# Row-tile outputs, a PSUM-held output sum, K scores ahead of V scores and a new order of transfers in an attention and feed-forward backward step

## The chip, the cores and the metric

One Trainium2 chip, one of its cores. The metric is the device time of one execution in microseconds; each quoted time is the median of several executions. The traced execution is a separate one, and its span lies some 1 to 5 us under the timed median. In what follows PE is the matrix engine, DVE and ACT are the vector and the scalar engine, and SP and Pool are the two engines that issue transfers here (Pool also does some small computation). PSUM is the memory that PE's products are written to; DVE and ACT copy them out of it (`evac` in the code).

## The reference

The forward pass is one decode step, one new token for each of four sequences, with attention over a sliding window of a cache and a GEGLU feed-forward block in parallel. The kernel computes the output and its gradients for x, both caches and all weights.

```python
# B=4, D=512, Hq=32, Hkv=8, Sk=4096, Dh=128, F=1792, W = 1024 (the window), bf16
xn = layernorm(x)
q  = (xn @ wq)                                    # 32 heads, 4 of them on each cached head
k, v = k_cache[:, :, Sk-W:], v_cache[:, :, Sk-W:]
o  = softmax(q k^T / sqrt(Dh)) v
y  = x + o @ wo + (gelu(xn @ w_gate) * (xn @ w_up)) @ w_down
# outputs: y, and the gradients for x, k_cache, v_cache, wq, wo, w_gate, w_up, w_down
```

The gradients of the caches have the full length of 4096 positions, but only the last 1024 are other than zero. So three quarters of dK and dV are plain zeros that the kernel has to write: 32 stores of 1536 KB, 50 MB of the 81 MB written.

## The kernel before

Attention runs in four rounds `t` of two cached heads each. In a round, K and V blocks are transposed on PE for the scores (`T_ps`, `S_ps`, `dP_ps`), a softmax follows, then o and dq (`od_ps`), the dV and dK products (`kv_ps`) with their stores, and the weight gradients dwo and dwq with theirs. The scores of round t+1 are computed between the dV and dK products and the weight gradients of round t. The order of SP's instructions is that of the program; the other engines' is the automatic scheduler's.

```python
# zeros and loads share SP's queue; each zero is held until a compute instruction is done
def zeros(n, after):
    for _ in range(min(n, len(zlist))):
        og, b, g = zlist.pop(0)
        z = nc.sync.dma_start(out=og[b, g:g + ZG, 0:K0, :]..., in_=zsrc)
        tc.add_manual_dep(z.ins, after.ins.name, ...)
...
def scores(t):                       # K and V together
    for b in range(B):
        for blk, nm in ((k_t[(t, b)], "k"), (v_t[(t, b)], "v")):
            ...  # 8 transposes into T_ps, ev = evac(T_sb, T_ps)
        zeros(1, ev)
        ...      # products into S_ps and dP_ps
...
def softmax(t):                      # one chain over both S_ps and dP_ps
    ...  # reduce_max -> PE (mT_ps) -> reduce_max -> PE (nm_ps) -> Exp, sums -> PE (tot_ps)
    ...  # -> P_b, dS_b -> PE (pT_ps) -> PT
...
def dvdk(t, stage):
    for src, mr, og, nm in ((P_b, domr, out_3, "dv"), (dS_b, qmr, out_2, "dk")):
        for g in range(GP):
            ...  # 8 products into kv_ps, ev = evac(stg, kv_ps)
            nc.gpsimd.dma_start(out=og[...], in_=stg[...])
        zeros(1, ev)
...
def fin(t):
    ao_ps = ps_x.tile([B, D], FP32, name="ao_ps", tag="x")       # sums on 4 partitions
    for h in range(HG):
        nc.tensor.matmul(ao_ps[:], lhsT=oT[:, h, :], rhs=wo_sb[:, h, :], start=(h == 0), stop=(h == HG - 1))
    nc.vector.tensor_tensor(out=acc_o[:], in0=ao_ps[:], in1=acc_o[:], op=ALU.add)
    ...  # transposes of o and dq to [4, 1024], the same for dxa_ps
    ...  # dwo and dwq products, contraction over 4 rows, stores on Pool
...
for t in range(NT):
    softmax(t)
    odq(t)
    ...  # loads for t+1 and t+2, pre(t+1)
    dvdk(t, stage)
    if t + 1 < NT:
        scores(t + 1)
    fin(t)
```

Of the kernel before, what the change touches and what calls it, by code (L numbers as in the profile page):

```python
# [13 lines left out]
P = 128  # L14
# [3 lines left out]
def kernel(  # L18
# [57 lines left out]
    ps_s = ctx.enter_context(tc.tile_pool(name="ps_s", bufs=1, space=bass.MemoryType.PSUM))  # L76
    ps_x = ctx.enter_context(tc.tile_pool(name="ps_x", bufs=2, space=bass.MemoryType.PSUM))
# [13 lines left out]
    x_b = const.tile([B, D], BF16, name="x_b")  # L91
    nc.sync.dma_start(out=x_b[:], in_=A_x.rearrange("b s d -> (b s) d"))
    dy_b = const.tile([B, D], BF16, name="dy_b")
    nc.sync.dma_start(out=dy_b[:], in_=grad_out.rearrange("b s d -> (b s) d"))
# [6 lines left out]
    nc.vector.memset(one_f[:], 1.0)  # L101

# [29 lines left out]
    x_f = const.tile([B, D], FP32, name="x_f")  # L132
    nc.vector.tensor_copy(out=x_f[:], in_=x_b[:])
    stats = const.tile([B, nc.vector.BN_STATS_DIM], FP32, name="stats")
    nc.vector.bn_stats(out=stats[:], in_=x_f[:])
    mv = const.tile([B, nc.vector.BN_AGGR_DIM], FP32, name="mv")
    nc.vector.bn_aggr(out=mv[:], in_=stats[:])
    eps_t = const.tile([B, 1], FP32, name="eps_t")
    nc.vector.memset(eps_t[:], eps)
    rstd = const.tile([B, 1], FP32, name="rstd")  # L140
    nc.scalar.activation(out=rstd[:], in_=mv[:, 1:2], func=ACT.Sqrt, bias=eps_t[:], scale=1.0)
    nc.vector.reciprocal(out=rstd[:], in_=rstd[:])
    xn_f = const.tile([B, D], FP32, name="xn_f")
    nc.vector.tensor_scalar(out=xn_f[:], in0=x_f[:], scalar1=mv[:, 0:1], scalar2=rstd[:, 0:1],
                            op0=ALU.subtract, op1=ALU.mult)
    xn_b = const.tile([B, D], BF16, name="xn_b")
# [4 lines left out]
    for src, dstT in ((dy_b, dyT), (xn_b, xnT)):  # L151
        tps = ps_x.tile([P, ND, B], BF16, name="tps", tag="x")
        for c in range(ND):
            nc.tensor.transpose(tps[:, c, :], src[:, c * P:(c + 1) * P], ident[0:B, 0:B])
        nc.vector.tensor_copy(out=dstT[:], in_=tps[:])


    acc_o = const.tile([B, D], FP32, name="acc_o")
    acc_d = const.tile([B, D], FP32, name="acc_d")
# [12 lines left out]
    def load_kv(t, bs):  # L172
        for b in bs:
            for d_, src, nm in ((k_t, A_k_cache, "kb"), (v_t, A_v_cache, "vb")):
                tl = kvp.tile([P, GP, J, Dh], BF16, name=nm, tag=nm)
                nc.sync.dma_start(
                    out=tl[:].rearrange("p g j d -> p g (j d)"),
                    in_=src[b, t * GP:(t + 1) * GP, K0:Sk, :].rearrange("g (m j) d -> m g (j d)", j=J))
                d_[(t, b)] = tl

# [4 lines left out]
    def zeros(n, after):  # L185

        zsrc = bass.AP(tensor=ztile.tensor, offset=ztile.offset, ap=[list(ztile[:].ap[0]), [0, ZG], [1, ZW]])
        for _ in range(min(n, len(zlist))):
            og, b, g = zlist.pop(0)
            z = nc.sync.dma_start(out=og[b, g:g + ZG, 0:K0, :].rearrange("g (m j) d -> m g (j d)", m=P), in_=zsrc)  # L190
            tc.add_manual_dep(z.ins, after.ins.name,
                              mybir.DependencyInfo(mybir.DependencyClass.Sync, mybir.DependencyReason.DATA))
# [4 lines left out]
    def pre(t):  # L197

        wo_sb, wq_sb = wo_t[t], wq_t[t]
        do_ps = ps_x.tile([P, HG, B], FP32, name="do_ps", tag="x")  # L200
        for h2 in range(HG // 2):
# [4 lines left out]
            woT = tsb.tile([P, 2, ND, P], BF16, name="woT", tag="wT", bufs=2)  # L206
            evac(woT[:], wT_ps[:], 1024, half=True)
            for i in range(2):
                for c in range(ND):
                    nc.tensor.matmul(do_ps[:, 2 * h2 + i, :], lhsT=woT[:, i, c, :], rhs=dyT[:, c, :],  # L210
                                     start=(c == 0), stop=(c == ND - 1))
        q_ps = ps_x.tile([P, HG, B], FP32, name="q_ps", tag="x")
        for h in range(HG):
            for c in range(ND):
                nc.tensor.matmul(q_ps[:, h, :], lhsT=wq_sb[:, c, h * Dh:(h + 1) * Dh], rhs=xnT[:, c, :],
                                 start=(c == 0), stop=(c == ND - 1))
        res = []
        for ps, sc, zt, nm in ((do_ps, None, dom_all[t % 2], "do"), (q_ps, scale, qm_all[t % 2], "qs")):
            xT4 = attw.tile([P, NQ, B, HG], BF16, name=nm + "T4", tag=nm + "T4")
            src = ps[:].rearrange("p h b -> p b h").unsqueeze(1).broadcast_to([P, NQ, B, HG])  # L220
            if sc is None:
                nc.vector.tensor_copy(out=xT4[:], in_=src)
            else:
# [3 lines left out]
            r_ps = ps_x.tile([P, P], BF16, name=nm + "r_ps", tag="x")  # L227
            nc.tensor.transpose(r_ps[:], xT4[:].rearrange("p q b h -> p (q b h)"), ident[:])
            r4 = attw.tile([P, Dh], BF16, name=nm + "_r4", tag=nm + "_r4")
            nc.vector.tensor_copy(out=r4[:], in_=r_ps[:])  # L230
            mr = attw.tile([P, GP, B, Dh], BF16, name=nm + "mr", tag=nm + "mr")
            nc.gpsimd.tensor_tensor(out=mr[:].rearrange("p g b d -> p (g b) d"),  # L232
                                    in0=r4[:].unsqueeze(1).broadcast_to([P, NS, Dh]),
                                    in1=msk[:].rearrange("p g b -> p (g b)").unsqueeze(2).broadcast_to([P, NS, Dh]),
                                    op=ALU.mult)
            res.append(mr)
        st[t] = res

    def scores(t):
        qm_f = qm_all[t % 2][:].rearrange("p s c -> p (s c)")  # L240
        dom_f = dom_all[t % 2][:].rearrange("p s c -> p (s c)")
        S_ps = ps_s.tile([P, WQ], FP32, name="S_ps", tag="S")
        dP_ps = ps_s.tile([P, WQ], FP32, name="dP_ps", tag="dP")
        for b in range(B):
            tiles = []
            for blk, nm in ((k_t[(t, b)], "k"), (v_t[(t, b)], "v")):
                for g in range(GP):
                    T_ps = ps_w.tile([P, J, P], BF16, name="T_ps", tag="w")
                    for j in range(J):
                        nc.tensor.transpose(T_ps[:, j, :], blk[:, g, j, :], ident[:])  # L250
                    T_sb = tsb.tile([P, J * P], BF16, name="T_sb", tag="T" + nm)
                    ev = evac(T_sb[:], T_ps[:].rearrange("p j m -> p (j m)"), 1024, half=True)
                    tiles.append(T_sb)
            zeros(1, ev)
            for i, (acc, lf) in enumerate(((S_ps, qm_f), (dP_ps, dom_f))):
                for g in range(GP):
                    s = b * GP + g
                    for q in range(NQ):
                        nc.tensor.matmul(acc[q * RG:(q + 1) * RG, :], lhsT=lf[:, s * RG:(s + 1) * RG],  # L259
                                         rhs=tiles[i * GP + g][:, q * WQ:(q + 1) * WQ],  # L260
                                         start=(s == 0), stop=(s == NS - 1), tile_position=(0, q * RG))
        st[t] += [S_ps, dP_ps]

    def softmax(t):
        domr, qmr, S_ps, dP_ps = st[t]
        m = attw.tile([P, 1], FP32, name="m", tag="m")
        nc.vector.reduce_max(out=m[:], in_=S_ps[:], axis=AX.X)
# [12 lines left out]
        sums = attw.tile([P, 2], FP32, name="sums", tag="sums")  # L280
        nc.scalar.activation(out=E_f[:], in_=S_ps[:], func=ACT.Exp, bias=negm[:, 0:1], scale=1.0,
                             accum_out=sums[:, 0:1])
        Gt = attw.tile([P, WQ], FP32, name="Gt", tag="Gt")
        nc.vector.tensor_tensor_reduce(out=Gt[:], in0=E_f[:], in1=dP_ps[:], scale=1.0, scalar=0.0,  # L284
                                       op0=ALU.mult, op1=ALU.add, accum_out=sums[:, 1:2])
        tot_ps = ps_x.tile([P, 2], FP32, name="tot_ps", tag="x")
        nc.tensor.matmul(tot_ps[:], lhsT=rsum[:].rearrange("p q r -> p (q r)"), rhs=sums[:], start=True, stop=True)  # L287
        rr = attw.tile([P, 1], FP32, name="rr", tag="rr")
        nc.vector.reciprocal(out=rr[:], in_=tot_ps[:, 0:1])
        cc = attw.tile([P, 1], FP32, name="cc", tag="cc")  # L290
        nc.vector.tensor_tensor(out=cc[:], in0=tot_ps[:, 1:2], in1=rr[:], op=ALU.mult)
        P_b = attw.tile([P, WQ], BF16, name="P_b", tag="P_b")
        nc.scalar.activation(out=P_b[:], in_=E_f[:], func=ACT.Copy, scale=rr[:, 0:1])
        nc.vector.scalar_tensor_tensor(out=Gt[:], in0=dP_ps[:], scalar=cc[:, 0:1], in1=E_f[:],
                                       op0=ALU.subtract, op1=ALU.mult)
        dS_b = attw.tile([P, WQ], BF16, name="dS_b", tag="dS_b")
        nc.vector.tensor_scalar(out=dS_b[:], in0=Gt[:], scalar1=rr[:, 0:1], scalar2=None, op0=ALU.mult)

        pT_ps = ps_x.tile([P, 2, JQ, P], BF16, name="pT_ps", tag="x")
        for i, src in enumerate((P_b, dS_b)):  # L300
            for jj in range(JQ):
                nc.tensor.transpose(pT_ps[:, i, jj, :], src[:, jj * P:(jj + 1) * P], ident[:])
        PT = attw.tile([P, 2, JQ, P], BF16, name="PT", tag="PT")
        evac(PT[:], pT_ps[:], 512, half=True)
        st[t] = [domr, qmr, P_b, dS_b, PT]

    def odq(t):
        domr, qmr, P_b, dS_b, PT = st[t]
        od_ps = ps_x.tile([P, 2, NS, rep], FP32, name="od_ps", tag="x")
        for i, blks in enumerate((v_t, k_t)):  # L310
            for b in range(B):
                for g in range(GP):
                    s = b * GP + g
                    for j in range(J):
                        q, jj = j // JQ, j % JQ
                        nc.tensor.matmul(od_ps[:, i, s, :], lhsT=blks[(t, b)][:, g, j, :],  # L316
# [288 lines left out]
```

## Time and profile before

| | before |
|---|---|
| time, median of the first 3 runs | 328.48 us |
| traced span | 325.5 us |
| PE busy | 243.0 us (75%) |
| bytes moved by DMA | 112.08 MB, mean 344 GB/s |
| DMA idle, summed over slices of 4 us | 37.5 us |

The profile's rows themselves are read in the prediction.

### The profile page before, as it was taken

To read this page: it belongs to the slowest core of one execution; us is meant where nothing else is said; L and a number is where in the kernel's file an instruction comes from. 1 tells how busy PE (TensorE), PEld (TensorE's weight loads), DVE (VectorE), ACT (ScalarE), POOL (GpSimd) and SP (SyncE) were. 2 spreads that over 40 slices of the span, in tenths; PEclk is the share of its full clock that TensorE was granted. 3 is DMA by queue.
4 is the path that set the end of the run, shared out by engine and by line. 5 is a ranking of instruction groups with operands and counts; after the bars stand their busy time and mean duration, and the time that the engine had idled before them with its cause. 6 is when DMAs were issued, how large, how long until landed. Compare 5 with 4: busy or idle time off the path is not lost.

```text
span 325.5 us, 6244 instructions
## 1 busy us (share of the span) xinstructions
PE 243.0 (75%) x2630; PEld 135.7 (42%) x2630; DVE 158.6 (49%) x308; ACT 131.2 (40%) x202; POOL 51.5 (16%) x76
## 2 busy tenths in 40 slices
PE   0459986677997999980529999926199999269990
PEld 0355542226875337720425167315151674142430
DVE  5134353554465574662105666703055766156684
ACT  3013353444552564451105545611065556135651
POOL 6000002221400520020003310110024101101111
PEclk9999996555797557975555559955575599555595
DMA  6999999688596999999999899999976999983726
GB/s 237 381 365 386 383 393 423 280 322 353 231 406 273 340 418 425 418 423 411 375 339 385 329 376 404 411 377 396 324 281 239 382 399 413 387 313 142 280 110 244
DMA packets 34411, 112.08 MB, mean 344 GB/s; under 512 B 1920, under 2 KB 7824, under 8 KB 34384
## 3 DMA queue, kind: packets, MB, share of 16 engines
q1 hardware_dynamic: 26576, 81.02, 65.1%
q0 software_dynamic: 7808, 30.67, 24.7%
q8 instruction: 20, 0.33, 0.4%
q14 instruction: 7, 0.06, 0.0%
HBM read 30.68 MB, written 81.01 MB: 343 GB/s over the span
## 4 chain that ended last, share of the span: by engine, by line
PE 57%; DMA 30%; issue 4%; ACT 4%; DVE 4%; SPq 0%; ACTq 0%; DVEq 0%; POOLq 0%
DMA wo_sb<-in_A_wo_dram 15%; PE T_ps L250 12%; PE kv_ps L337 11%; DMA wd_sb<-in_B_w_down_dram 5%; PE ao_ps L352 5%; DMA out_dram<-osb_o 4%; PE woT_ps L205 4%; DMA out_dram<-osb_d 3%; DMA out_dram<-osb_g 3%; PE dxf_ps L496 2%; PE wqT_ps L369 2%; PE od_ps L316 2%; PE dP_ps L259 2%; PE dxa_ps L374 2%; PE S_ps L259 2%
## 5 line engine op out<-in xcount | busy, mean ns | idle before, releaser
L88 ACT COPY T_sb<-T_ps 128x1024 bf16<-128x1024 bf16 x26 | 26.1, 1013 | 26.4 <-PE T_ps L250 26.4
L89 DVE COPY T_sb<-T_ps 128x1024 bf16<-128x1024 bf16 x38 | 25.8, 690 | 19.6 <-PE T_ps L250 19.3
L205 PE MATMUL woT_ps<-ident,wo_sb 128*128 128x128 bf16 x128 | 13.7, 282 | 16.1 <-DMA wo_sb<-in_A_wo_dram 16.1
L89 DVE CAST stg_dk<-kv_ps 128x512 bf16<-128x512 f32 x30 | 20.7, 691 | 9.8 <-PE kv_ps L337 9.5
L88 ACT CAST stg_dv<-kv_ps 128x512 bf16<-128x512 f32 x34 | 19.3, 588 | 14.5 <-PE kv_ps L337 14.3
L250 PE MATMUL T_ps<-ident,kb 128*128 128x128 bf16 x256 | 24.8, 247 | 0.0
L89 DVE CAST stg_dv<-kv_ps 128x512 bf16<-128x512 f32 x30 | 20.1, 688 | 8.8 <-PE kv_ps L337 8.5
L88 ACT CAST stg_dk<-kv_ps 128x512 bf16<-128x512 f32 x34 | 19.5, 587 | 10.7 <-PE kv_ps L337 10.1
L337 PE MATMUL kv_ps<-domr,P_b 32*128 32x512 bf16 x64 | 20.5, 562 | 0.9 <-DVE stg_dv L89 0.7
L337 PE MATMUL kv_ps<-qsmr,dS_b 32*128 32x512 bf16 x64 | 20.8, 600 | 0.0
L287 PE MATMUL tot_ps<-sums,rsum 128*128 128x2 f32 x8 | 2.0, 323 | 24.9 <-DVE sums L284 24.9
L250 PEld LDWEIGHTS <-kb 128*128 128x128 bf16 x256 | 17.9, 111 | 6.6 <-issue 4.2
L89 DVE CAST osb_q<-dwq_ps 128x512 bf16<-128x512 f32 x16 | 10.4, 683 | 19.9 <-DMA out_dram<-osb_o 19.4
L250 PE MATMUL T_ps<-ident,vb 128*128 128x128 bf16 x256 | 20.1, 240 | 0.0
L352 PE MATMUL ao_ps<-wo_sb,oT 128*4 128x512 bf16 x32 | 18.6, 589 | 0.0
L89 DVE COPY woT<-woT_ps 128x1024 bf16<-128x1024 bf16 x10 | 6.9, 692 | 23.5 <-PE woT_ps L205 23.0
L205 PEld LDWEIGHTS <-wo_sb 128*128 128x128 bf16 x128 | 11.1, 128 | 17.4 <-DMA wo_sb<-in_A_wo_dram 16.3
L250 PEld LDWEIGHTS <-vb 128*128 128x128 bf16 x256 | 18.0, 110 | 0.1
L88 ACT CAST osb_q<-dwq_ps 128x512 bf16<-128x512 f32 x16 | 8.8, 587 | 19.3 <-DMA out_dram<-osb_o 18.7
L88 ACT COPY woT<-woT_ps 128x1024 bf16<-128x1024 bf16 x6 | 6.1, 1012 | 25.6 <-PE woT_ps L205 22.3
L386 POOL DMA_DIRECT2D out_dram<-osb_o x8 | 6.0, 754 | 65.4 <-ACT osb_o L88 57.2
L232 POOL TENSOR_TENSOR domr<-do_r,msk 128x1024 bf16<-128x1024 bf16 x4 | 7.6, 1891 | 47.6 <-DVE do_r L230 47.6
(184 smaller groups left out, 420.3 us busy)
## 6 DMA issues: line engine op xcount, KB each, us to landing
out_dram<-ztile SPq DMA_DIRECT2D x32, 1536.0 KB, 14.4
kb<-in_A_k_cache_dram SPq DMA_DIRECT2D x16, 512.0 KB, 11.1
vb<-in_A_v_cache_dram SPq DMA_DIRECT2D x16, 512.0 KB, 11.1
out_dram<-stg_dv POOLq DMA_DIRECT2D x8, 1024.0 KB, 6.5
out_dram<-stg_dk POOLq DMA_DIRECT2D x8, 1024.0 KB, 8.8
wo_sb<-in_A_wo_dram SPq DMA_DIRECT2D x4, 1024.0 KB, 12.5
wq_sb<-in_A_wq_dram SPq DMA_DIRECT2D x4, 1024.0 KB, 20.2
out_dram<-osb_o POOLq DMA_DIRECT2D x8, 512.0 KB, 9.6
```

Of the source, the lines that this page charges most:

```text
L88: return nc.scalar.copy(out=out, in_=in_)
L89: return nc.vector.tensor_copy(out=out, in_=in_)
L205: nc.tensor.transpose(wT_ps[:, i, c, :], wo_sb[:, 2 * h2 + i, c * P:(c + 1) * P], ident[:])
L232: nc.gpsimd.tensor_tensor(out=mr[:].rearrange("p g b d -> p (g b) d"), in0=r4[:].unsqueeze(1).broadcast_to([P, NS, Dh]), in1=msk[:].rearra ...
L250: nc.tensor.transpose(T_ps[:, j, :], blk[:, g, j, :], ident[:])
L259: nc.tensor.matmul(acc[q * RG:(q + 1) * RG, :], lhsT=lf[:, s * RG:(s + 1) * RG], rhs=tiles[i * GP + g][:, q * WQ:(q + 1) * WQ], start=(s = ...
L316: nc.tensor.matmul(od_ps[:, i, s, :], lhsT=blks[(t, b)][:, g, j, :], rhs=PT[:, i, jj, q * RG + s * rep:q * RG + (s + 1) * rep], start=(j = ...
L337: nc.tensor.matmul(mps[:].rearrange("p b d -> p (b d)"), lhsT=src[rs, jj * P:(jj + 1) * P], rhs=mr[rs, g].rearrange("p b d -> p (b d)"), s ...
L352: nc.tensor.matmul(ao_ps[:], lhsT=oT[:, h, :], rhs=wo_sb[:, h, :], start=(h == 0), stop=(h == HG - 1))
L369: nc.tensor.transpose(wT_ps[:, i, c, :], wq_sb[:, c, h * Dh:(h + 1) * Dh], ident[:])
L374: nc.tensor.matmul(dxa_ps[:], lhsT=dqT[:, h, :], rhs=wqT[:, i, :], start=(h == 0), stop=(h == HG - 1))
L496: nc.tensor.matmul(dxf_ps[:], lhsT=srcT_b[:, fc, :], rhs=wgT[:, i, :], start=(w_ == 0 and fc == 0), stop=(w_ == 1 and fc == NF - 1))
```

## The change

Its intent, part by part:

- **o and dq as row tiles:** the products that give o and dq put their rows on 128 partitions (four groups of 32, four rows used in each), where before they gave columns that had to be transposed to 4 partitions.
- **Masked full-array products:** dwo, dwq and the feed-forward weight gradients contract over 128 rows, with all rows but the four wanted ones masked to zero in `xnm` and `dym`.
- **Output sums in PSUM:** the sums for y and dx stay in one PSUM tile `acc_ps` to the end of the kernel, in products of 4 columns.
- **K scores, then V:** the softmax is cut in two, so that P and the o products need not wait for the V scores.
- **Transfers:** SP only loads. The zeros go to Pool's queue, in program order among the stores, without a gate of their own. Two of them wait for the last V load of round 0.

The transposes of w_gate and w_up now come behind the weight-gradient products of the feed-forward part; before, they came first. Besides, the pool `ps_x` of small PSUM tiles goes from two buffers to one, and x and dy are loaded 32 times over, on 128 partitions.

```diff
 def zeros(n, after=None):
-            z = nc.sync.dma_start(out=og[b, g:g + ZG, 0:K0, :]..., in_=zsrc)
+            z = nc.gpsimd.dma_start(out=og[b, g:g + ZG, 0:K0, :]..., in_=zsrc)
 ...
-        load_kv(0, range(B))
-        load_kv(1, range(2))
-        load_w(1)
+        last = load_kv(0, range(B))
+        load_w(1)
+        load_kv(1, range(2))
+        zeros(2, last)
 ...
+        def ftb(name):
+            t_ = ffn.tile([P, 4 * NF4, B], BF16, name=name)
+            nc.gpsimd.memset(t_[:], 0.0)
+            return t_
 ...
+    def acc_add(o, c, lhsT, rhs):
+        nc.tensor.matmul(acc_ps[:, o, c, :], lhsT=lhsT, rhs=rhs, start=False, stop=False)
 ...
-            nc.tensor.matmul(ao_ps[:], lhsT=oT[:, h, :], rhs=wo_sb[:, h, :], start=(h == 0), stop=(h == HG - 1))
+            for c in range(ND):
+                acc_add(0, c, wo_sb[:, h, c * P:(c + 1) * P], oT[:, h // rep, h % rep, :])
 ...
-                nc.tensor.matmul(mps[:], lhsT=o_bp[:, h * Dh:(h + 1) * Dh], rhs=dy_b[:], start=True, stop=True)
+                nc.tensor.matmul(mps[:], lhsT=o_r[:, g, :], rhs=dym[:, i, :], start=True, stop=True)
 ...
         pre(0)
-        scores(0)
+        masks(0)
+        scores(0, 0)
+        softmax(0)
+        scores(0, 1)
+        softmax_d(0)
         for t in range(NT):
-            softmax(t)
-            odq(t)
+            odq(t, 0)
+            odq(t, 1)
 ...
-            dvdk(t, stage)
-            if t + 1 < NT:
-                scores(t + 1)
+            dvdk(t, 0, stage)
+            if nxt:
+                scores(t + 1, 0)
+                softmax(t + 1)
+            dvdk(t, 1, stage)
+            if nxt:
+                masks(t + 1)
+                scores(t + 1, 1)
+                softmax_d(t + 1)
             fin(t)
 ...
+        zeros(len(zlist))
```

## The prediction

> **What bounds the kernel now.** I read first the slices of the page, to see which unit is full when; then the totals of the DMA queues; then the chain that ended last; then the busy table by stage, cut where the chain changes its kind.
>
> ```profile
> span 325.5 us, 6244 instructions
> ...
> PE   0459986677997999980529999926199999269990
> ...
> PEclk9999996555797557975555559955575599555595
> DMA  6999999688596999999999899999976999983726
> GB/s 237 381 365 386 383 393 423 280 322 353 231 406 273 340 418 425 418 423 411 375 339 385 329 376 404 411 377 396 324 281 239 382 399 413 387 313 142 280 110 244
> DMA packets 34411, 112.08 MB, mean 344 GB/s; under 512 B 1920, under 2 KB 7824, under 8 KB 34384
> ```
>
> The PE row has holes (the 0, the 2, the 1) where the DMA row is at 9. The DMA row has holes of its own: at the start, in slices 8 to 13 (56 to 104 us), near slice 31, and in the last five. 112.08 MB at the 344 GB/s mean is the span; at the 390 to 420 of full slices it would be 267 to 287 us. So the transfers are the floor, and the loss is the time in which they are not fed.
>
> ```profile
> DMA wo_sb<-in_A_wo_dram 15%; PE T_ps L250 12%; PE kv_ps L337 11%; DMA wd_sb<-in_B_w_down_dram 5%; PE ao_ps L352 5%; DMA out_dram<-osb_o 4%; PE woT_ps L205 4%; DMA out_dram<-osb_d 3%; DMA out_dram<-osb_g 3%; PE dxf_ps L496 2%; PE wqT_ps L369 2%; PE od_ps L316 2%; PE dP_ps L259 2%; PE dxa_ps L374 2%; PE S_ps L259 2%
> ```
>
> The largest member of the chain is the load of wo, 15% of 325.5 = 49 us: two pieces, 25.3 us from 143.5 and 23.8 us from 211.4 in the chain by time. The wo of the round after next stands on the one SP queue behind eight zero stores of 1536 KB each.
>
> ```profile
> 2.50:48.00 45.50, 30.91 (x409) 19.86 (x409) 17.54 (x47) 12.11 (x15) 3.51 (x13) 1.00 1.05 375
> 48.00:80.00 32.00, 22.65 (x105) 9.79 (x104) 14.89 (x26) 13.96 (x24) 7.52 (x12) 0.54 0.85 344
> 80.00:112.00 32.00, 29.64 (x508) 21.21 (x505) 17.95 (x42) 14.59 (x22) 6.40 (x5) 0.77 0.82 313
> 112.00:143.00 31.00, 30.52 (x284) 16.48 (x284) 19.37 (x31) 17.15 (x25) 4.89 (x6) 0.78 1.03 418
> 143.00:169.00 26.00, 7.26 (x143) 5.53 (x142) 4.60 (x14) 3.24 (x8) 2.18 (x3) 0.50 1.00 380
> ...
> 288.00:325.50 37.50, 29.39 (x244) 12.06 (x244) 23.20 (x41) 16.99 (x30) 5.95 (x8) 0.59 0.55 203
> ```
>
> Columns: stretch, length, busy us of PE, PE weight load, DVE, ACT, POOL, then granted clock, DMA share, GB/s. From 143 to 169 PE works 7 of 26 us, yet DMA is at 1.00: PE waits for wo, but those bytes (zeros) have to go out at some time anyway. Only the shares under 1 are true loss. Summed over slices of 8 us, 1 minus the share comes to some 39 us, of which about 18 are after 288 us, some 20 between 56 and 104. **The bound is the DMA stream and how it is fed**, not PE's 75%.
>
> **What the skill says.** "DMA: Bandwidth & Descriptors", section "Issuing engines are not separate DMA queues": transfers of SP and GpSimd run on the same 16 engines and interleave; a second issuer saves only issue time. So moving the zeros to Pool buys no bandwidth, only a different order. The trace agrees: the two queues took 65.1% and 24.7% for 81.02 and 30.67 MB, the same share per byte. "TensorE: Matmul & The Clock Gate", section "LDWEIGHTS (loading the stationary operand)": weight time follows the columns, not the rows. Agrees: 4x128 weights of xn_b take 106 ns where 128x128 take 104 to 111, so a masked product with all 128 rows costs no more than its 4-row form. The same page, Part 1: the default clock is half, and activity releases it. The trace has 1.00 in the dense start and 0.50 in the stretches where PE waits; I take no saving from it, as those are not PE's to set. "PSUM — Partial Sum Buffer", "The four PSUM rules": matmuls without the first flag keep adding to a written element, which lets one bank hold both sums to the end; no run here tests it.
>
> **The change part by part.**
>
> *Output sums.* ao, dxa, dxf and fo are 32+32+28+14 products with 512 moving columns: in the chain by time ao takes 0.52 us each, the others 0.26. That is 16.6 + 8.3 + 7.3 + 3.6 = 36 us. In their place come 4 products of 4 columns each, 424 in all, at the pace of the 128 od products (3.46 us, 27 ns): 12 us. About 24 us off PE. Eight DVE adds of 0.67 us (5 us) go too.
>
> *Row tiles.* The 64 + 42 transposes of tq and tf and their copies on 4 partitions (up to 1.0 us each, some 12 us over DVE and ACT) go; 16 transposes, 48 small products and small copies come. Some 7 us off PE. dwo, dwq, dwd and dwg keep their moving columns and their evacuations (0.59 us ACT, 0.68 DVE). od stays at 64 issues a side.
>
> Together about 30 us of PE work and 15 us of evacuation go, but nearly all of it in rounds that end waiting for transfers, so it is not 30 us of time.
>
> *Order of transfers.* The bytes stay at about 112.4 MB (the x and dy broadcasts add 0.25). Three things move:
> 1. Loads are alone on SP. wo of round t is now read early in the PE order, so the next wo leaves well ahead. The 49 us of PE waits go; PE then waits for store buffers instead, where it outruns the DMA.
> 2. Two zeros at the start wait for the last V load of round 0. They sit on the in-order Pool queue, and **the three memsets of aT_b, dhuT_b and dhgT_b sit behind them**. From the issue times before (one 512 KB load per 1.36 us) that load lands at about 36 us; so the FFN products start at about 40 us, not at 27 as their operands would let them (before, dwd started at 46).
> 3. Zeros stand between stores. None can leave while Pool waits for the next store, so between the last FFN store and the first dV store **nothing feeds the DMA**.
>
> *Time line.* (a) Loads on SP: 16.5 MB at 375 GB/s from 2.5 us: to 46.5. (b) Behind them 2 zeros (3.15 MB), FFN stores (5.5 MB) and 6 zeros (9.4 MB): 18 MB at 420, as full store slices show: 43 us, to 90 us. (c) PE is held by the three output buffers: its 12th FFN tile may fill once the 9th has landed, 13.6 MB into (b), at 79 us. From there it has the last transposes of w_up (5 us), pre(0) (5), scores (14 for K and V before, 81.7 to 95.5), the two softmax parts (6, part hidden), od (3): about 33 us, to 112. The DMA is empty from 90 to 112: **a 22 us hole**. (d) From 112 the remaining 77.5 MB. At 387 (time-weighted mean of the four stretches from 112 to 235 us) 200 us, less 3 because the last round's 15.7 MB are stores alone at 420: 197. (e) Inside the rounds compute and DMA are close: 22 MB or 56 us of DMA against some 45 to 50 us of compute; I allow 2 us for gaps. (f) 2 us for the last landing. Sum 112 + 197 + 2 + 2 = 313 us of span.
>
> A check from the other side: idle before about 39; after it 2.5 + 22 + 2 + 2 = 28.5, so 325.5 - 10.5 = 315. The timed runs lie 3.0 above the traced span (328.48 against 325.5), so 313 gives 316; I choose **315**, since the end of the last round may be fed better than I allowed.
>
> **Rivals.**
> *The hole is filled or shorter* (PE reaches dV sooner because the full-row products hold the clock at 1.00 and 30 us of work is gone): for it, slices 0 to 6 ran at 1.00 with dense work; against it, PE is held by the output buffers until 79 us whatever its speed. A hole of 8 us gives 301.
> *The in-order Pool queue becomes the bound*: every store waits for all ahead of it, zeros included, with 3 output and 4 stage buffers. For it, the chain already has out_dram<-osb_o at 4%, osb_d and osb_g at 3% each, with one zero now between. Against it, a wait behind a zero is time in which DMA works. If each round loses 4 us to it: 329.
> *The gain of PE is passed on in full* (if PE were the bound, 49 + 30 us: 250): against it, 112.4 MB in 250 us would need 450 GB/s and no full slice shows more than 425.
> *Compute bounds the rounds*: splitting the softmax in two adds a dependency chain (E_f, rr, P_b, then Gt, cc, dS_b). At 56 us a round: 325.
>
> **Range and chances.** The floor, with 2.5 us of start and no hole, is 112.4 MB / 397 (full slices) = 283 + 5, and 291 timed; I don't believe in it, as the hole follows from the queue order. Low 300 (half the hole), high 328 (rounds lose another 3 us each). Over 2% faster means under 321.9: 0.72. Within 2%: 0.22. Slower: 0.06.
>
> **What would show each step.** The chain no longer has 15% of wo loads, and PE's wait for wo is near 0. Sum products of 4 columns cost about 27 ns each. Pool's memsets of aT_b end at 35 to 40 us, and dwd starts after 38. The DMA row has a hole of two or three slices between 85 and 115 us, and is at 9 from there to the end, where slices 36 to 40 were 2 to 8. PE's waits move to the osb buffers, that is to stores behind zeros. The prediction is wrong if the hole is absent, if full slices run below 370 GB/s with the zeros on the software queue, if the rounds after 112 us show DMA gaps of over 10 us in all, or if Pool's issues take much more than the 0.75 us of before.

## More of the kernel before

The trace gives the mean busy share of the 16 DMA engines for any stretch; I cut the span into slices of 4 us, the last one ending with the span, and add up (1 minus the share) times the length, counting shares over 1 as 1. It says how long the DMA engines stood unfed.

(The idle times and the "281 us" that some expectations quote were summed with a last slice that ran past the end of the span, by up to 3.8 us.)

## The result and the profile after

The changed kernel is correct and **slower**: 338.97 us median (337.38 to 340.69, 4 runs) against 328.21 us (327.5 to 328.7) on the same chip. The ratio is 1.0331, with a 95% interval of 1.0275 to 1.0386. A ratio here is the mean time of one kernel's fast runs over that of the other's of the same rounds, so not quite the ratio of the medians.

From the page of the changed kernel: span, busy tenths and bytes in 40 slices of 8.4 us, the two DMA queues, and the chain that ended last.

```profile
span 335.5 us, 6853 instructions
...
PE   1352182477977899698669689768959988990020
...
DMA  5999999997900079887999999599998938999995
GB/s 175 395 361 385 373 417 418 420 417 312 411 26 2 12 259 380 352 337 301 350 415 418 416 413 410 216 358 416 417 419 347 395 149 325 376 395 403 405 389 211
...
q0 software_dynamic: 16512, 81.01, 59.9%
q1 hardware_dynamic: 18120, 30.94, 26.3%
...
PE T_ps L279 13%; DMA out_dram<-osb_o 12%; PE kv_ps L374 10%; PE S_ps L284 4%; DMA wq_sb<-in_A_wq_dram 4%; DMA out_dram<-osb_g 4%; DMA vb<-in_A_v_cache_dram 3%; PE wqT_ps L395 3%; PE woT_ps L233 3%; SPq L193 3%; PE acc_ps L146 3%; DMA out_dram<-osb_d 3%; PE wgT_ps L555 3%; PE od_ps L348 3%; DVE T_sb L90 2%
```

The 15% of wo loads are gone from the chain, the tail of the DMA row is all but full (slices 36 to 40 were 2 to 8 before), and a hole of three slices stands at 92 to 118 us. All of this was foreseen. What was not are the weak places among the rounds: slices 17 to 19, 26, 31, 33 and 34. The idle DMA time is 51.1 us against 37.5 before, 13.6 more, and the span is 10.0 longer.

Pool's timeline of the changed kernel shows the hole from the side of the issuer. Columns: start, duration, engine, line, operation, count; in brackets how long Pool waited before it, and for what.

```profile
38.89 1.59 POOL L217 DMA_DIRECT2D out_dram<-ztile  x2 [33.11 <-DMA vb<-in_A_v_cache_dram]
40.48 0.17 POOL L458 MEMSET aT_b<- 128x64 bf16 x1
...
84.37 0.71 POOL L217 DMA_DIRECT2D out_dram<-ztile  x1
...
123.92 0.80 POOL L378 DMA_DIRECT2D out_dram<-stg_dv  x1 [26.04 <-ACT stg_dv L89]
...
142.44 0.78 POOL L378 DMA_DIRECT2D out_dram<-stg_dk  x1 [8.10 <-ACT stg_dk L89]
...
159.98 0.79 POOL L409 DMA_DIRECT2D out_dram<-osb_o  x1 [8.74 <-ACT osb_o L89]
```

The last zero of the feed-forward part leaves at 84.4 and the first dV store at 123.9. Between them Pool issues no transfer at all, though 24 zeros are still in its program: each stands behind a store that is not ready. After that the three groups of stores of round 0 are 18.5 and 17.5 us apart.

### The profile page after: what moved, and what is told of

Read it like the earlier page. It is cut to its first block, busy times and chain, and to the rows that moved or that the text cites. A ratio compares the mean times of both kernels' runs of the same rounds, so it can differ in the third digit from the quotient of the medians.

```text
span 335.5 us, 6853 instructions
## 1 busy us (share of the span) xinstructions
PE 223.8 (67%) x2956; PEld 142.8 (43%) x2956; DVE 154.4 (46%) x304; ACT 127.7 (38%) x203; POOL 74.3 (22%) x111
## 4 chain that ended last, share of the span: by engine, by line
PE 50%; DMA 26%; DVE 9%; ACT 5%; SPq 4%; issue 3%; POOL 1%; ACTq 0%; DVEq 0%; POOLq 0%
PE T_ps L279 13%; DMA out_dram<-osb_o 12%; PE kv_ps L374 10%; PE S_ps L284 4%; DMA wq_sb<-in_A_wq_dram 4%; DMA out_dram<-osb_g 4%; DMA vb<-in_A_v_cache_dram 3%; PE wqT_ps L395 3%; PE woT_ps L233 3%; SPq L193 3%; PE acc_ps L146 3%; DMA out_dram<-osb_d 3%; PE wgT_ps L555 3%; PE od_ps L348 3%; DVE T_sb L90 2%
## 5 line engine op out<-in xcount | busy, mean ns | idle before, releaser
L90 DVE COPY T_sb<-T_ps 128x1024 bf16<-128x1024 bf16 x40 | 27.7, 692 | 31.5 <-PE T_ps L279 31.3
L89 ACT COPY T_sb<-T_ps 128x1024 bf16<-128x1024 bf16 x24 | 24.3, 1012 | 31.2 <-PE T_ps L279 25.0
L217 POOL DMA_DIRECT2D out_dram<-ztile x32 | 22.8, 714 | 50.1 <-DMA vb<-in_A_v_cache_dram 33.1
L279 PE MATMUL T_ps<-ident,vb 128*128 128x128 bf16 x256 | 24.4, 258 | 0.0
L374 PE MATMUL kv_ps<-qmr,dS_b 32*128 32x512 bf16 x64 | 22.6, 596 | 0.3
L89 ACT CAST stg_dk<-kv_ps 128x512 bf16<-128x512 f32 x33 | 18.9, 587 | 7.1 <-PE kv_ps L374 6.7
L279 PEld LDWEIGHTS <-kb 128*128 128x128 bf16 x256 | 18.9, 115 | 5.3 <-issue 3.1
L374 PE MATMUL kv_ps<-domr,P_b 32*128 32x512 bf16 x64 | 18.6, 528 | 2.1 <-DVE stg_dv L90 0.8
L378 POOL DMA_DIRECT2D out_dram<-stg_dv x8 | 6.2, 775 | 45.6 <-ACT stg_dv L89 44.0
L600 PE MATMUL f_ps<-ident_f,acc_r 128*128 128x128 f32 x8 | 2.0, 428 | 20.3 <-ACT osb_q L89 20.3
L378 POOL DMA_DIRECT2D out_dram<-stg_dk x8 | 6.2, 779 | 40.0 <-ACT stg_dk L89 28.9
L233 PEld LDWEIGHTS <-wo_sb 128*128 128x128 bf16 x128 | 10.2, 119 | 10.5 <-issue 10.3
L89 ACT CAST osb_d<-dwd_ps 128x512 bf16<-128x512 f32 x8 | 4.6, 587 | 25.4 <-PE dwd_ps L529 18.6
```

Of the source, the lines that this page charges most:

```text
L89: return nc.scalar.copy(out=out, in_=in_)
L90: return nc.vector.tensor_copy(out=out, in_=in_)
L217: z = nc.gpsimd.dma_start(out=og[b, g:g + ZG, 0:K0, :].rearrange("g (m j) d -> m g (j d)", m=P), in_=zsrc)
L233: nc.tensor.transpose(wT_ps[:, i, c, :], wo_sb[:, 2 * h2 + i, c * P:(c + 1) * P], ident[:])
L279: nc.tensor.transpose(T_ps[:, j, :], blks[(t, b)][:, g, j, :], ident[:])
L374: nc.tensor.matmul(mps[:].rearrange("p b d -> p (b d)"), lhsT=src[rs, jj * P:(jj + 1) * P], rhs=mr[rs, g].rearrange("p b d -> p (b d)"), s ...
```

## The experiments

Where only the zeros or the program order were edited, the automatic scheduler also moved some instructions of PE, DVE and ACT. All results were correct. The same-round kernel before had medians of 328.15, 326.64, 327.19 and 327.29 us in the four batches, which ran on three chips; so a difference between runs of different batches is good to some 1.5 us. For e4, e6, e9 and e14 the interval of the ratio contains 0.98 but ends below 1: they are faster than before, by about 2%.

| run | what it is | median us | ratio to before | span | DMA idle us |
|---|---|---|---|---|---|
| before | | 328.21 | 1 | 325.5 | 37.5 |
| after | the change | 338.97 | 1.0331 | 335.5 | 51.1 |
| e1_fill | after, six zeros moved into the hole | 332.72 | 1.0138 | 330.2 | 44.1 |
| e2_memset | after, memsets ahead of the two zeros | 339.10 | 1.0350 | 336.2 | 51.8 |
| e3_oldqueue | compute of after, zeros on SP with gates | 327.27 | 0.9981 | 323.3 | 37.3 |
| e4_newqueue_before | compute of before, transfers of after | 322.63 | 0.9828 | 321.8 | 39.2 |
| e5_dxfirst | e2, w_gate and w_up transposes first | 337.62 | 1.0312 | 335.9 | 51.0 |
| e6_kvtogether | after, K and V scores together | 320.95 | 0.9806 | 317.7 | 36.5 |
| e7_both | e5 and e6 | 313.86 | 0.9586 | 312.5 | 31.5 |
| e8_bothfill | e7, eight zeros moved into the hole | 314.27 | 0.9605 | 313.2 | 29.0 |
| e9_beforefill | e4, the same move | 320.19 | 0.9758 | 318.2 | 32.9 |
| e10_splitspread | after, a zero of each pair held to mid-scores | 338.71 | 1.0333 | 335.5 | 50.7 |
| e11_best | e7, seven zeros in the hole, the others regrouped | 304.01 | 0.9279 | 301.5 | 18.9 |
| e12_oldq_together | e3, K and V scores together | 314.25 | 0.9575 | 309.7 | 25.2 |
| e13_joinstores | after, dV and dK side by side, chain in the middle | 338.04 | 1.0288 | 336.4 | 53.8 |
| e14_movechain | after, softmax moved behind the V scores | 319.35 | 0.9754 | 316.8 | 36.0 |

### First batch: the hole, the memsets, and compute against queue order

Theory H: the hole after the feed-forward part costs the time, and the order of transfers is at fault. Its rivals were that Pool's single queue binds (P), and that the new compute does (C).

**e1_fill**

```diff
-            if f4 % 2: zeros(1)             # and the same among the w_gate, w_up stores
+        zeros(1, ev)                        # after the last w_up transpose
+            if t == 0 and h2 == 1: zeros(1, ev)                    # in pre
+                if t == 0 and b % 2 and g == GP - 1: zeros(1, ev)  # in scores
```

> The changed kernel, with the six zero stores that stood between the FFN stores moved into the stretch of round 0 without any store (one behind the last w_up transpose, one in pre(0), four in the scores of round 0, each gated on an evacuation). Theory H (the hole between the last FFN store and the first dV store, about 27 us with a DMA share near 0, sets the loss): the FFN buffers come free some 15 us sooner (6.3 MB less ahead of the 9th store, at 0.42 MB per us) and the hole is mostly filled, so 320 us, between 315 and 326, against 339. Rival P (the zeros between the stores of the rounds hold the in-order Pool queue, the hole only lies beside it): 333 or more.

Measured 332.72 us, 1.0138 (1.0087 to 1.019). It falls between the two: 6 us came back, not enough to reach the kernel before. The trace shows that the run moved the hole more than it filled it: from 88 to 124 us the idle DMA time fell from 25.0 to 6.0 us, but from 56 to 84, where the six zeros had been, it rose from 1.9 to 13.4. So e1 doesn't say what a filled hole is worth, and it leaves open whether the hole makes the change a loss; e4 settles that.

**e2_memset**

```diff
+        for name in ("aT_b", "dhuT_b", "dhgT_b"):
+            t_ = ffn.tile([P, 4 * NF4, B], BF16, name=name)
+            nc.gpsimd.memset(t_[:], 0.0)
         zeros(2, last)
```

> The changed kernel, with the three memsets on Pool ahead of the two zeros that wait for the last V load. Theory H: the FFN products start some 13 us sooner, but the stores stay behind the same zeros and the DMA is full until 72 us anyway, so under 4 us is gained: 335 to 339. Rival M (the late FFN start is handed on to everything after it): 326, that is 13 us less.

Measured 339.10 us, 1.035 (1.0285 to 1.0414). The memsets behind the zeros really held PE for 12.9 us, and it cost nothing: the products for y that use `aT_b` start at 27.0 us instead of 41.0, but the first dV store leaves at 124.3 where it was 123.9.

**e3_oldqueue**

```diff
-            z = nc.gpsimd.dma_start(out=og[b, g:g + ZG, ...
+            z = nc.sync.dma_start(out=og[b, g:g + ZG, ...
-                evac(stg[:, :, j, :], mps[:], 512)
+                ev = evac(stg[:, :, j, :], mps[:], 512)
-            zeros(1)
+        zeros(1, ev)               # and the other gates as in the kernel before
```

> The computation of the changed kernel, with the zeros on the SP queue behind gates on evacuations, 8 a round and 5 in the FFN, as in the kernel before; Pool has only stores. Theory H (the order of transfers is at fault, the new computation saves some time): no hole, 318 us, between 312 and 325, under the 328 of before. Rival C (the new computation is at fault, by its split softmax and its longer PE order): 335 or more, like the changed kernel.

Measured 327.27 us, 0.9981 (0.9918 to 1.0044). Neither theory: the new compute under the old queue order gains nothing and loses nothing.

**e4_newqueue_before**

```diff
-            z = nc.sync.dma_start(out=og[b, g:g + ZG, ...
+            z = nc.gpsimd.dma_start(out=og[b, g:g + ZG, ...
-            zeros(1, ev)
+                zeros(1)           # one behind each store, as in the changed kernel
+    def masks(t):                  # the mask products leave pre: Pool's order is now fixed
```

> The computation of the kernel before, with the transfers of the change: loads alone on SP, the zeros on Pool between the stores in the same places, two behind the last V load (this kernel has no memsets behind them). Theory H: it gets the hole and the short round gaps too, 345 us, between 338 and 355, slower than before by 3% or more. Rival C (the order of transfers is harmless or good): 330 or less.

Measured 322.63 us, 0.9828 (0.9773 to 0.9883). H is refuted: the new order of transfers alone makes the old compute 1.7% faster, hole and all (its slices 12 and 13 moved 22 and 2 GB/s, and it has 19.8 us of idle DMA from 88 to 124). So the loss is in the compute part, or in how the two go together.

### Second batch: which part of the compute

Theory R: two things delay the stores. One is that the w_gate and w_up transposes stand behind buffer-bound products, so the first dV store is late; the other is the split of K and V.

**e5_dxfirst**

```diff
+        for srcT, wsb in ((dhgT_b, wg_sb), (dhuT_b, wu_sb)):
+            ...                    # transposes and acc_add(1, ...), moved up unchanged
         def f_rows(srcT, nm):
-            for f2 in range(NF // 2):
-                ...                # from behind the w_gate and w_up stores
```

> The kernel of e2 (memsets ahead of the zeros), and the transposes of w_gate and w_up with their sums put ahead of the FFN weight gradients, as in the kernel before, in place of among and behind them. Theory T (what the change lost is the time to the first dV store, as nothing is sent until then and some 214 us follow it in the changed kernel, in e1 and in e4; a part of that delay is the PE work that waits behind FFN products held by the output buffers): round 0 starts some 8 us sooner, 331 us, between 327 and 334. Rival R (the time after the first dV store is what counts, and takes up any shift): 337 to 341, like e2.

Measured 337.62 us, 1.0312 (1.0277 to 1.0347). The first dV store leaves at 119.7 instead of 123.9, but the next round's at 180.4, where it was 179.8: the rounds swallow the gain.

**e6_kvtogether**

```diff
-        scores(0, 0); softmax(0); scores(0, 1); softmax_d(0)
+        scores(0, 0); scores(0, 1)
         for t in range(NT):
+            softmax(t)
+            softmax_d(t)
 ...
-                scores(t + 1, 0); softmax(t + 1)
             dvdk(t, 1, stage)
-                masks(t + 1); scores(t + 1, 1); softmax_d(t + 1)
+                masks(t + 1); scores(t + 1, 0); scores(t + 1, 1)
```

> The changed kernel with K and V scores together and the two softmax parts after both, as before. Theory T: the chain of the first softmax part stands between the K and the V transposes on the in-order PE, and the stage from the wo transposes to the first dV product takes 33 us against 24.5 in e4; undone, the first dV store comes about 8 us sooner and the rounds are not longer: 330 us, between 324 and 334. Rival R (the split costs nothing, since V transposes run beside the chain): 336 or more.

Measured 320.95 us, 0.9806 (0.9767 to 0.9844). 18 us came back by the order of the calls alone: same instructions, same transfers. The first dV store is where it was (124.0 against 123.9), so an earlier first store is not the reason; the gain lies in the rounds.

**e7_both**

> e5 and e6 in one: what is left of the change is row tiles, masked products, the one PSUM accumulation and the queue order. Theory T: the two delays add up, and the first dV store comes as early as in e4 or a few us sooner: 320 us, between 313 and 326, within 2% of e4's 322.6. Rival A (the row tiles, masked products or PSUM sums cost time themselves): 330 or more, clearly above e4.

Its edit is the two above together. Measured 313.86 us, 0.9586 (0.9539 to 0.9632). With the rounds repaired, the feed-forward order that was worth nothing in e5 is worth 7 us (e6 to e7).

**e8_bothfill**

```diff
+                if t == 0 and g == GP - 1: zeros(1, ev)     # in scores
-        zeros(1)                   # the two in fin
```

> e7, with eight zeros moved out of the rounds (the two of each fin) into the scores of round 0, each behind an evacuation there. Theory T: the hole of some 25 us gets 12.6 MB (30 us of DMA) that the rounds then lack, so 300 us, between 292 and 308. Rival B (the rounds are bound by the computation, so bytes taken from them buy nothing): 315 or more.

Measured 314.27 us, 0.9605 (0.9567 to 0.9642), a miss. The hole shrank from 22 us to 6, but the zeros taken from `fin` left new gaps ahead of the dV stores and at the end: from 140 to 280 us the idle DMA time rose from 2.0 to 12.5.

### Third batch: where zeros are of use, and the split under the old queue

**e9_beforefill** (the edit of e8 on e4)

> e4 (the computation of before, the transfers of the change) with the two zeros of each round's fin moved into the scores of round 0, as e8 has them against e7. e8 gained nothing (314.3 against 313.9): it closed the hole of round 0 but had new gaps before the dV stores and at the end, as fin no longer has a zero. Theory G (the span is 281 us, give or take 4, of full transfers plus the time in which the DMA is not fed, whatever the computation): e9 too wins the hole and loses it in the rounds: 318 to 325. Rival (a filled hole is worth its length): 303.

Measured 320.19 us, 0.9758 (0.9695 to 0.9821), 2.4 us under e4: inside the range of theory G and far from the rival's 303.

**e10_splitspread**

```diff
+                if t > 0 and b == 1 and g == GP - 1: zeros(1, ev)   # in scores
-            zeros(1)
+            if g == 0 or t == NT - 1: zeros(1)
```

> The changed kernel, K then V kept, with one of the two zeros behind each pair of dV stores and of dK stores held back until the middle of the K scores and of the V scores of the next round (gated on an evacuation). Theory G: the round gaps of the split (about 16 us of DMA idle between 136 and 280 us) come from the queue running dry while PE does scores and softmax; spread zeros fill them: 325 us, between 319 and 330. Rival S (the split's softmax chain on the PE order sets the rounds, and the gaps only show it): 335 or more.

Measured 338.71 us, 1.0333 (1.028 to 1.0385): nothing. That is in the range of rival S, but it was a poor test, as I saw in the trace. The second zero of the dV pair already left late in the changed kernel (at 133.6), so my gate moved the same bytes in the same order by a few microseconds.

**e11_best**

```diff
+            if t == 0 and h2 == 1: zeros(1, ev)                                 # in pre
+                if t == 0 and g == GP - 1 and (k == 0 or b < 2): zeros(1, ev)   # in scores
-            zeros(1)               # behind each dV and dK store
+            if t + 1 < NT: zeros(1)
-        zeros(1)                   # in fin, behind the dwo stores
-        zeros(1)                   # in fin, behind the dwq stores
+        zeros(1 if t + 1 < NT else len(zlist))
```

> e7 with seven zeros in the hole (one in pre(0), six in the scores of round 0), one zero behind the last store of each fin but the last, and in the last round none between the stores and two behind all of them. Theory G: the hole is closed and neither the rounds nor the end run dry; DMA idle falls from 35 to about 14 us: 298 us, between 291 and 306. Rival S (the rounds are bound by computation): 310 or more.

Measured **304.01 us**, 0.9279 (0.9224 to 0.9334), which beats both kernels. Its page, busy tenths of DMA and GB/s in 40 slices of 7.5 us:

```profile
DMA  5999999999998999996999999999999999679696
GB/s 151 399 350 384 381 386 418 422 422 417 414 417 338 400 425 380 361 416 277 340 400 418 412 348 359 422 418 393 411 406 405 421 414 406 241 308 362 250 349 266
```

No empty slice is left. What remains lies in the first slice, slice 19 and the last six; 18.9 us of idle DMA against 31.5 in e7.

**e12_oldq_together** (the edit of e6 on e3)

> e3 (the computation of the change, zeros on SP behind gates as before) with K and V scores together. Theory S (the split lengthens the PE path of each round by the softmax chain, under any order of transfers): 314 us, between 308 and 320, so 7 or more under e3's 327.3. Rival Q (the split only hurts together with zeros on Pool, since gated zeros fill its stretches): 323 or more.

Measured 314.25 us, 0.9575 (0.9512 to 0.9637): 13 us under e3. So the split costs under the old queue too, and it isn't an effect of zeros on Pool.

### Fourth batch: what in the split costs

Joining K and V does two things at once: it takes the softmax chain of K out from between two blocks of scores, and it puts the dV and dK products and stores side by side. Two runs take these apart.

**e13_joinstores**

```diff
-                scores(t + 1, 0); softmax(t + 1)
             dvdk(t, 1, stage)
                 masks(t + 1)
+                scores(t + 1, 0); softmax(t + 1)
                 scores(t + 1, 1); softmax_d(t + 1)
```

> The changed kernel with the dV and dK products of a round back to back again, and their stores with them, while the K scores, their softmax chain and the V scores stay split after them. Theory C (the split costs because the chain of the K softmax stands in PE's order between two blocks of scores): no gain, 335 to 342 us. Theory S (the split costs because the dV and the dK stores of a round are pulled apart, so that the stores and the zeros behind them come late): most of the 18 us comes back, 319 to 326 us. In between, 327 to 334: both have a part.

**e14_movechain**

```diff
         for t in range(NT):
+            softmax(t)
+            softmax_d(t)
 ...
-                scores(t + 1, 0); softmax(t + 1)
+                scores(t + 1, 0)
             dvdk(t, 1, stage)
-                masks(t + 1); scores(t + 1, 1); softmax_d(t + 1)
+                masks(t + 1); scores(t + 1, 1)
```

> The changed kernel with its order dV, K scores, dK, V scores kept, but both softmax chains moved behind the V scores to the head of the next round, as in the kernel that had K and V together. Theory C: the 18 us come back, 319 to 326 us. Theory S: no gain, 335 to 342 us. With the run beside it and the two that are there, all four pairings of (stores joined or apart) with (chain in the middle or behind) are measured.

Measured 338.04 us (1.0288, 1.0202 to 1.0374) and 319.35 us (0.9754, 0.9701 to 0.9806). All four pairings are now there:

| | softmax in the middle of the round | softmax behind the V scores |
|---|---|---|
| dV and dK apart | after 338.97 | e14 319.35 |
| dV and dK side by side | e13 338.04 | e6 320.95 |

Rows differ by under 2 us, columns by 17 to 20. **The place of the softmax chains, with what moves along with them, costs the whole 18 us; the place of the stores costs nothing.** The hole is the same in all four (25 to 26 us of idle DMA from 88 to 124), and so the 18 us lie in the rounds. Nor is it the clock: the traced executions of e13 and e6 both had a mean granted clock (the share of PE's full speed that was granted) of 0.758. The traces show in part how it comes about. PE's timeline in round 0 of the changed kernel:

```profile
134.60 0.27 PE L303 MATMUL mT_ps<-ident_f,m 128*1 128x128 f32 x1 [0.53 <-DVE m L301]
135.58 0.35 PE L310 MATMUL nm_ps<-one_f,mx 1*128 1x1 f32 x2 [0.71 <-DVE mx L307]
136.78 0.42 PE L317 MATMUL es_ps<-es,rsum 128*128 128x1 f32 x2 [0.85 <-ACT E_f L315]
138.07 0.39 PE L293 MATMUL pT_ps<-ident,P_b 128*128 128x128 bf16 x2 [0.86 <-ACT P_b L321]
...
154.92 1.56 PE L395 MATMUL wqT_ps<-ident,wq_sb 128*128 128x128 bf16 x25
```

The same of e14, from the V transposes to the softmax:

```profile
137.08 2.51 PE L279 MATMUL T_ps<-ident,vb 128*128 128x128 bf16 x22
...
144.92 0.33 PE L395 MATMUL wqT_ps<-ident,wq_sb 128*128 128x128 bf16 x3
...
148.81 0.27 PE L303 MATMUL mT_ps<-ident_f,m 128*1 128x128 f32 x1
...
152.94 0.38 PE L310 MATMUL nm_ps<-one_f,mx 1*128 1x1 f32 x2
```

In the changed kernel, four tiny PE operations alternate with steps of DVE and ACT, and PE waits at each (the brackets: 0.53, 0.71, 0.85, 0.86). Nothing else runs on PE from 134 to 138, though the dK products stand ready behind them (in e14 they start at 132.0). "TensorE: Matmul & The Clock Gate" of the Trainium skill, Part 3, section "The mechanism", says that matmuls start and end in program order, without reordering; the trace agrees, for no matmul passes the waiting one. In e14 the first two of these steps come among the dwo and dwq products, and PE waits for neither (no bracket). The wq transposes start at 144.9 instead of 154.9, and the first dwo store leaves at 150.4 instead of 160.0.

PE's waits over the three later rounds (130 to 280 us) of the changed kernel, by what it waited for: total us, times, longest.

```profile
PE woT_ps L233 <- ACT osb_q L89: 10.1, 2, 5.9
PE pT_ps L293 <- ACT P_b L321: 2.6, 3, 0.9
PE es_ps L317 <- ACT E_f L315: 2.5, 3, 0.8
PE nm_ps L310 <- DVE mx L307: 2.1, 3, 0.7
PE pT_ps L293 <- DVE dS_b L337: 1.9, 3, 0.6
```

And of e14 (125 to 265 us):

```profile
PE pT_ps L293 <- ACT osb_q L89: 16.0, 3, 6.7
PE es_ps L317 <- ACT E_f L315: 2.5, 3, 0.8
...
PE gs_ps L331 <- DVE rr L319: 0.8, 3, 0.3
```

With the smaller groups (mT_ps 1.6, gs_ps 1.1, odT_ps 0.7) the softmax holds PE for 12.5 us in the changed kernel and for 3.3 in e14, whose long wait (16.0) is one for output buffers, that is, for the DMA to take the stores away: there ACT's copy into osb_q, behind which the next softmax step stands on ACT, waits 13.6 us, in three turns, for dwo stores to land. In that kernel PE runs ahead of the DMA, in the changed one behind it. That shows in the busy table by stage. Columns as in the prediction: stretch, length, busy us of PE, PE weight load, DVE, ACT, POOL, granted clock, DMA share, GB/s. The changed kernel, in the hole and in four weak places of the rounds:

```profile
96.00:104.00 8.00, 4.49 (x56) 3.03 (x55) 3.32 (x8) 2.51 (x5) 1.88 (x2) 0.93 0.00 1
...
136.00:144.00 8.00, 6.36 (x44) 1.68 (x44) 4.35 (x8) 5.35 (x11) 1.48 (x2) 0.56 0.71 292
...
152.00:160.00 8.00, 6.37 (x118) 4.42 (x106) 5.30 (x13) 3.67 (x6) 0.02 (x1) 1.00 0.76 285
...
208.00:220.00 12.00, 10.23 (x153) 7.46 (x151) 7.26 (x16) 5.55 (x9) 0.99 (x3) 0.86 0.71 272
...
264.00:280.00 16.00, 14.43 (x243) 10.51 (x239) 9.32 (x18) 7.32 (x11) 4.67 (x5) 0.89 0.60 231
```

And e14, the last four stretches:

```profile
136.00:144.00 8.00, 7.88 (x78) 5.52 (x76) 3.90 (x7) 3.49 (x5) 6.70 (x6) 0.60 1.02 409
...
152.00:160.00 8.00, 2.09 (x14) 1.59 (x14) 2.42 (x9) 1.44 (x4) 1.81 (x3) 0.76 0.99 337
...
208.00:220.00 12.00, 5.33 (x128) 4.62 (x131) 3.83 (x9) 1.77 (x4) 1.42 (x2) 0.61 1.03 415
...
264.00:280.00 16.00, 14.52 (x216) 7.93 (x216) 12.14 (x22) 11.12 (x21) 6.28 (x9) 0.71 0.91 357
```

From 208 to 220 the changed kernel has PE busy for 10.2 of 12 us and the DMA at 0.71; e14 has PE busy for 5.3 and the DMA at 1.03. From 140 us to 280 the DMA stands unfed for 15.8 us in the changed kernel and for 1.8 in e14 (sums of 4 us slices); in e13 for 16.9, in e6 for 1.4.

What stays open: the waits differ by 9 us, while the kernels differ by nearly 20. The timeline shows one candidate for the rest. With P ready early, the o products of the next round are issued amid this round's dK products and V transposes (from 139.4 and from 151.5 on), ahead of the dwo products that feed the next store. No run separates that from the waits. Nor does a run move one softmax chain alone: of the 12.5 us of waits, 8.8 belong to the chain behind the K scores and 3.7 to the one behind the V scores.

## Why the prediction was wrong

The prediction was 315 us with 300 to 328; it came to 339. Step by step:

- **The bound is the DMA stream and how it is fed: right.** Spans and idle times of all runs bear it out (span less idle is 284 us to within 4). Its reading of the idle time was wrong in the parts: by its own shares (0.85 of 32 us, 0.82 of 32 us) the stretch from 48 to 112 us loses 10.6 us, not some 20 between 56 and 104; 5.1 us near 244 us are not named; and 2.5 of the 39 lie past the end of the span.
- **Sums and row tiles: right in kind, small in effect.** The 424 sum products cost 16.7 us of PE where 12 were estimated; PE's busy time fell by 19 us (243.0 to 223.8), not by 30. The loads of 128-row weights from `xnm` took 97 and 113 ns where those of 4-row weights from `xn_b` had taken 106 and 126 (the prediction read only the 106), so they cost no more, as foreseen. As foreseen, this is not time by itself. Row tiles, masked products and the PSUM sum together are worth 9 us when nothing else spoils them (e4 322.63 to e7 313.86, which differ in these, and in small things beside: three memsets, K loads ahead of V loads, and the scheduler's moves).
- **Transfer order, 1: right.** The wo waits went, from 15% of the chain; PE waits for buffers at that place. The rates held (most slices full of stores moved 395 to 420 GB/s), and Pool issues took 0.54 to 0.87 us.
- **Transfer order, 2: right and harmless.** The zeros left at 38.9 and the memsets ran at 40.5, against 36 and 40 predicted. e2 shows that it costs nothing.
- **The hole, (b) and (c): right in kind, 5 us too short.** Predicted 90 to 112, measured 92 to some 117. It was loads that ended it, those of K and V for round 1, issued from 115.9 us on; the first dV store, which (c) had at 112, left only at 123.9. Small slips, of a us or two, are in the bytes: the loads of the start come to 16.2 MB, not 16.5, and 78 MB are left after (b), not 77.5.
- **(e), "Inside the rounds compute and DMA are close … I allow 2 us for gaps": this step failed.** The gaps from 140 to 280 us are 15.8 us, where 2 were allowed. The estimate compared 56 us of DMA with "some 45 to 50 us of compute", a sum of busy times. But PE's path in a round also holds the waits of its softmax steps, and the split places them where nothing may overtake them: 12.5 us of such waits, against 3.3 in e14. What the rest of the loss is made of stays open, as said above. The prediction had named the sign itself: gaps "of over 10 us in all" after 112 us. The distances between the first dV stores of successive rounds are 56, 59 and 46.5 us, where e14, with the chains moved, has 54, 52 and 43.

My idle sum was 28.5 us (2.5 start, 22 hole, 2 gaps, 2 end). Measured: 3.6 at the start, 1.9 near 76 us, 25.9 for the hole and its edge, 15.8 in the rounds, 4.0 at the end, in all some 51. Of the 23 us of difference the rounds are 14 and the hole is 4.

The rival *Compute bounds the rounds* named the cause, the dependency chain of the split softmax, and priced it at 325. What it named was right and its size was too small; I gave it too little weight, since I judged PE idle time harmless when the DMA is the bound. It is harmless only as long as stores are ready. The rival of the in-order Pool queue as the bound is not borne out: e4 has the same queue and is faster than the kernel before. Of the clock, which it left out of the sum, the prediction read only one side: the kernel before was granted 0.50 not only where PE waits, but also from 112 to 120 us and from 248 to 256, where PE was busy for all 8 us.

The parts of the change, as a ladder under the new transfer order:

| step | median us | difference |
|---|---|---|
| before | 328.21 | |
| new transfer order only (e4) | 322.63 | -5.6 |
| with row tiles, masked products, PSUM sums (e7) | 313.86 | -8.8 |
| with the new place of the w_gate and w_up transposes and of the memsets (e6) | 320.95 | +7.1 |
| with K scores, then V (after) | 338.97 | +18.0 |

Each step from batch to batch carries the 1.5 us of above. The steps do not simply add: the third is worth 7 us here but under 2 us with the split in place (after 338.97, e2 339.10, e5 337.62). And the change's net under the old queue order is near zero because a gain of 13 us (e12, 314.25 against 327.19) and a loss of 13 us by the split (e12 to e3) cancel.

## What to carry to other kernels

In this kernel a softmax whose small steps alternate between engines held PE at each step, unless independent work stood between those steps in PE's program; so before splitting or moving such a chain, look at what will stand right behind it, not only at how early its result would be there. When transfers are the floor, count the time in which the DMA is unfed, and ask of every reordering when the next store becomes ready. Filler transfers such as these zeros are best kept for stretches without stores: placing seven of 32 in one such hole and regrouping the rest brought 10 us (e7 to e11), while eight taken out of `fin` alone brought nothing (e7 to e8).

## What the Trainium skill lacked or had wrong

- "DMA: Bandwidth & Descriptors", section "Issuing engines are not separate DMA queues", says that a second issuing engine saves only issue time. The rates bear it out: no slice of the page moved more than 425 GB/s before, and none more than 420 after, with the zeros on the other queue. That section lacks that the choice of queue also decides which waits a transfer stands behind: the same bytes under the new order took 322.63 us instead of about 328 (e4).
- No page says in so many words that a queue of stores in program order leaves ready transfers unissued behind a store that isn't ready: 24 zeros waited while the DMA moved 26, 2 and 12 GB/s in slices 12 to 14 of the changed kernel. Moving six zeros there gave 6 us back (e1), though they left gaps of 13.4 us where they came from.
- No page gives a figure for what a chain of small steps across engines costs an engine whose matmuls keep their order: one softmax of four PE steps held PE for about 3 us of waits (0.53 + 0.71 + 0.85 + 0.86), and moving these chains brought 338.97 us to 319.35.
